# Blocks 2 to 6 of a fused attention and MLP layer: the second norm by row group, heads normalized by pairs, no held-back products

## The chip, the core and the metric

The kernel runs on one core of a Trainium2 chip. Its engines work from queues of their own, each in order: PE (TensorE, with its weight loads as PEld), DVE (VectorE), ACT (ScalarE), POOL (GpSimd), and SP, which issues nearly all transfers. They meet through semaphores. The metric is the device time of one execution in microseconds (us). The kernel before takes 1557.15 us, the median of three runs (1557.05 to 1557.82).

## The reference, cut to what matters

Sequence 2048, width 512, 32 heads of width 16 with one key and one value head for all, MLP width 1376.

```python
mod = silu(c) @ w_mod                       # six rows of 512: sa, ca, ga, sb, cb, gb
h = layernorm(x) * (1 + ca) + sa
q, k, v = h @ wq, h @ wk, h @ wv            # 32 query heads, one k and one v of width 16
p = softmax(q @ k.T / 4)                    # per head, 2048 x 2048
x = x + ga * ((p @ v) @ wo)
h = layernorm(x) * (1 + cb) + sb            # "the second norm"
x = x + gb * (gelu(h @ w1 + b1) @ w2 + b2)
```

Everything is fp32. Where a product of the projections and the MLP is made, each factor is split into a high and a low part in fp32r, and three matmuls (high by high, low by high, high by low) are summed; below, each of these matmuls counts as one product.

## The kernel before, in words

**Blocks, units, iterations.** The 2048 query rows are worked off in 8 blocks of 256 rows, numbered 0 to 7, and a block in 8 units of 4 heads. The main loop runs over the 64 units, four iterations to a unit: 256 iterations, 32 to a block. An iteration has two halves. In each half PE computes four score tiles transposed (`e`, line 615) for ACT to exponentiate (`p`, line 619), four score tiles in rows (`m`, line 510) of a unit some way ahead, of which DVE takes the maximum (`mx`, line 515), and at its end 16 matmuls of the probabilities with the values (`acc`, line 636). So two groups of 16 `acc` matmuls mark an iteration in the trace. The `e` and `m` tiles use 64 of the 128 rows of the array each, and two such matmuls can run side by side. From the 250th iteration on no `m` tiles are left; the loop then calls `alone`, and an iteration holds only `e`, `acc` and plain full-height matmuls. These are called the bare iterations.

**Batches.** What a block needs after its attention (the output projection, the second norm, the MLP) is written as a generator, `rest_steps`, which is fed into the iterations of the next block. It hands over batches of matmuls. One iteration takes at most one batch: six products of 512 columns (or twelve of 256), whose contraction is cut in two halves of 64 rows; one half runs beside the `e` and `m` tiles of the first half of the iteration, the other in the second. Batches of at most four products make an iteration of a shorter kind. An iteration without a batch is written by `plain`. The generator may also `yield` a number: it then rests for that many ticks of the variable `clock`, which counts four ticks to an iteration. `later(n, fn)` issues the instructions of `fn` after `n` ticks. Each engine's queue stands in the order that these calls give; nothing is moved afterwards.

**PSUM banks.** `m` tiles have three banks (tag "m"). A sum of the rest (`wops`, `tp`, `w1ps`, `w2ps`) has the bank "x". In an iteration without a batch, one `m` tile of each half goes to "x" (line 1447), so that four are then in use. A bank is free again when DVE has read it.

**The rest of a block, in order.** The output projection (`wops`) makes two row groups of 128 rows, two batches of six products in each of four iterations in all. DVE adds a row group to x (`add_x`, line 814). Then the second norm: `stats` (line 821, two instructions of 256 columns per row group), `rstd` (line 825: `bn_aggr` on DVE, line 827, then `ve`, line 828, and the power, line 830, on POOL), `xhat` on POOL (line 833), `add_bias` on POOL (line 837). In the kernel before, `rstd` is issued for both row groups together, and the generator rests 8 ticks, two iterations. Then two batches of four transposes (`tp`), the modulation on POOL, eleven tiles of the first MLP product (`w1ps`) with the gelu on DVE, ACT and POOL, and the second product (`w2ps`), 33 products for each of two row groups.

**Held-back products.** For blocks 4 and 5 (`held_back`, line 1045) the second row group stops 12 products short; the last 12 (`LATER = 4`) are made in two batches after the next block's output projection, in the two iterations in which that block's norm would otherwise leave none. A set `projected` says when.

**Heads.** Each head's sums must divide its outputs before the output projection. For blocks below `EARLY` this is done for the whole block after its last unit (`fetch`, line 726). From block `EARLY` on it is done by pairs of units while the block still runs (`finish_unit`, from line 664): `fetch_sums`, `invert_sums` (a reciprocal on DVE, line 676), `collect`, `scale_heads` on POOL (line 689). `EARLY` is 5 before.

**The end.** Block 6's last products are spread with `LONE` (how many of eleven k tiles of its first row group are made before the bare iterations) and batches of `SHORT` = 4 in the bare ones. What is left after the loop is given out by `some(n)` between the steps of block 7's norm: `TAIL[0]` products ahead of the first row group's transposes, `TAIL[1]` ahead of the second's, `TAIL[2]` ahead of the modulation.

Of the kernel before, what the change touches and what calls it, by code (L numbers as in the profile page):

```python
# [32 lines left out]
BUSY = 5  # L33
BATCH = 6
SHORT = 4
LONG = (3, 1)
TAIL = (11, 7, 6)
EARLY = 5
HELD = 4
LATER = 4  # L40
LONE = 5
SOON = 6
GROUP = 4
NORM_WAIT = 6
# [10 lines left out]
def adaln_mqa_mlp(  # L55
# [16 lines left out]
    _, S, D = x.shape  # L72
# [10 lines left out]
    NF = (F + P - 1) // P  # L83
# [710 lines left out]
    def rest_steps(b, fast, rp, bank, ons, ready):  # L794
# [4 lines left out]
        for hf in range(w // HQ):  # L799
# [20 lines left out]
            def stats(t, h):  # L820
                nc.vector.bn_stats(out=st[:, t, h, :], in_=x1[:, t, h * D // 2:(h + 1) * D // 2])  # L821
# [30 lines left out]
            if fast:  # L852
                turned = [psum.tile([P, HQ], F32, name=f"turned{q}", **bank()) for q in range(2)]
                rows_o = rp.tile([P, HQ], F32, name="rows_o", tag="rb", bufs=2)
                inv = att.tile([P, H * w // P], F32, name="inv", tag="rsum", bufs=1)

                def turn_o(q):
                    for t in range(2):
                        nc.tensor.transpose(turned[q][:, t * P:(t + 1) * P], ocs[q][:, t * P:(t + 1) * P], ident)

                def scale_o(q):
                    src = turned[q].rearrange("p (t c r) -> p t c r", t=2, c=4)
                    by = inv[:, 8 * q:8 * q + 8].rearrange("p (t c) -> p t c", t=2)
# [24 lines left out]
            else:  # L888
                for t in range(2):
                    ps = out_sum(t)  # L890
                    yield from batches(ps, out_pairs(t, range(KD)), BATCH, lambda g: b < EARLY or g in on_early[b][1])
                    add_x(t, ps)

                    for h in range(2):
                        later(3 - 2 * t + 2 * h, lambda t=t, h=h: stats(t, h))
                projected.add(b)
            if not fast:
                later(4, lambda: rstd(0, 2))
                later(5, lambda: xhat(0))
                later(5, lambda: xhat(1))  # L900
                later(9, lambda: add_bias(0))
                later(9, lambda: add_bias(1))

                later(BUSY, lambda: state.update(busy=True))
                yield 8
            hH = att.tile([P, KD, HQ], F32R, name=f"h2H{b}_{hf}", tag="xH", bufs=2)
            hL = att.tile([P, KD, HQ], F32R, name=f"h2L{b}_{hf}", tag="xL", bufs=2)

# [133 lines left out]

            while weights:
                yield 2
            held_back = not fast and EARLY <= b + 1 < len(blocks) - 1
            full = slice(0, D)
            parts = [(0, full), (1, slice(0, D // 2)), (1, slice(D // 2, D))] if fast else [(0, full), (1, full), (1, full)]
            sums = {}

            def second(n, fs, begin=True, end=True, put=store):  # L1050
                t, cols = parts[n]
                sl = slice(t * P, (t + 1) * P)
                if n not in sums:
                    place = dict(tag="m", bufs=3) if b == len(blocks) - 2 and t else bank()
                    sums[n] = psum.tile([P, D], F32, name=f"w2ps{b}_{hf}_{n}", **place)
                ops = [(gH[:, f, sl], gL[:, f, sl], w2H[:, f, cols], w2L[:, f, cols]) for f in fs]
                size_ = SHORT if b == len(blocks) - 2 and (t or not begin) else BATCH
                yield from batches(sums[n][:, :cols.stop - cols.start], ops, size_,
                                   lambda k: made.issuperset(range(fs[k] + 1)), begin, end)
                if not end:  # L1060
                    return
                if fast:
                    later(1, lambda: put(t, sums[n], cols))
                    yield 2
                else:
                    put(t, sums[n])
# [23 lines left out]
    projected = set()  # L1090
    drm = tc.dram_tile([4, D], F32, name="drm")

    mod_state = {}
# [487 lines left out]
```

## Time and profile before

| what | us |
|---|---|
| median of three runs | 1557.15 |
| the profiled execution | 1557.11 |
| its span, first to last instruction | 1555.3 |
| PE busy | 1539.4 (99%) |
| DVE busy | 1397.8 (90%) |
| ACT busy | 1230.8 (79%) |
| POOL busy | 685.5 (44%) |

The profiled execution's own time is 0.04 us below the median, so sums made against one hold for the other; 1.8 us of it lie around the span. The granted TensorE clock is 1.00 over the loop. A row of the timeline gives the start, how long it took, the engine, the line, the operation, what it writes and reads, and how many like instructions are merged in it (x2); in brackets stands how long the engine was idle ahead of it, and who released it. Matmuls overlap in the records: how fast PE goes is read from the distance between starts, not from the durations.

### The profile page before, as it was taken

What the parts mean: (1) busy time and instruction counts of PE and PEld (TensorE: products, weight loads), DVE (VectorE), ACT (ScalarE), POOL (GpSimd) and SP (SyncE); (2) the same over time, 40 slices, a digit from 0 to 9 for tenths busy, and PEclk for the clock granted to TensorE, in tenths of its full rate; (3) what the DMA queues carried; (4) which work ended last, traced back from release to release, by engine and by line L of the source; (5) the groups of instructions that cost most, each with busy time, mean ns of one, the idle gap of its engine ahead of it and who ended that gap; (6) DMA issues with size and microseconds to landing.
All of it is one profiled execution on the core that took longest, in us unless ns stands there. A gap on an engine that the chain in (4) does not pass through costs nothing.

```text
span 1555.3 us, 41563 instructions
## 1 busy us (share of the span) xinstructions
PE 1539.4 (99%) x16405; PEld 954.2 (61%) x16405; DVE 1397.8 (90%) x2488; ACT 1230.8 (79%) x2401; POOL 685.5 (44%) x1206
## 2 busy tenths in 40 slices
PE   7999999999999999999999999999999999999999
PEld 4455555567655665557655676556655676566658
DVE  7999999999999999999999999999999999999814
ACT  5577778788877887788877888788877888778874
POOL 5535432867322571246521563235711574046511
PEclk9999999999999999999999999999999999999999
DMA  7226412312030211203112120302102220202141
GB/s 248 94 88 200 151 57 83 127 51 97 18 106 25 74 67 37 93 19 109 33 51 79 56 87 16 111 26 93 62 31 73 65 96 24 87 28 99 48 150 48
DMA packets 84215, 120.85 MB, mean 78 GB/s; under 512 B 21342, under 2 KB 57438, under 8 KB 83764
## 3 DMA queue, kind: packets, MB, share of 16 engines
q1 hardware_dynamic: 84004, 118.18, 22.9%
q8 instruction: 130, 2.13, 0.6%
q14 instruction: 65, 0.53, 0.1%
q10 hardware_dynamic: 16, 0.00, 0.0%
HBM read 90.87 MB, written 26.74 MB: 76 GB/s over the span
## 4 chain that ended last, share of the span: by engine, by line
PE 90%; DVE 7%; DMA 1%; ACT 0%; issue 0%; POOL 0%; SPq 0%; ACTq 0%; DVEq 0%
PE acc L636 31%; PE m L510 25%; PE e L615 17%; PE w1ps L196 8%; DVE mx L515 6%; PE w2ps L186 2%; PE w2ps L196 2%; PE qps L196 1%; DMA xt<-in_A_x_dram 1%; PE w1ps L186 1%; PE wops L196 1%; PE tp L196 1%; PE kps L165 1%; DVE st L821 0%; DVE x L814 0%; PE wops L186 0%
## 5 line engine op out<-in xcount | busy, mean ns | idle before, releaser
L515 DVE TENSOR_REDUCE mx<-m 128x1 f32<-128x512 f32 x2048 | 1269.6, 681 | 88.1 <-PE m L510 65.0
L619 ACT ACTIVATE p<-e 128x512 f32<-128x512 f32 x2048 | 1099.0, 597 | 255.2 <-PE e L615 116.3
L510 PE MATMUL m<-ks,qst 64*128 64x512 f32 x2048 | 836.8, 429 | 2.0 <-DVE mx L515 0.6
L615 PE MATMUL e<-qst,ks 64*128 64x512 f32 x2048 | 740.4, 411 | 0.1
L636 PE MATMUL acc<-p,va 128*32 128x256 f32 x8192 | 548.0, 385 | 0.0
L510 PEld LDWEIGHTS m<-ks,qst 64*128 64x128 f32 x2048 | 367.4, 184 | 211.1 <-DVE mx L515 174.3
L615 PEld LDWEIGHTS e<-qst,ks 64*128 64x128 f32 x2048 | 359.3, 184 | 89.5 <-ACT p L619 61.8
L636 PEld LDWEIGHTS acc<-p,va 128*32 128x32 f32 x8192 | 213.8, 109 | 214.6 <-issue 111.6
L196 PE MATMUL w1ps<-h2H,w1t 64*128 64x256 f32 x1232 | 235.7, 287 | 0.0
L558 POOL TENSOR_SCALAR mt<-turned 8x32 f32<-8x32 f32 x256 | 53.3, 208 | 401.6 <-DVE turned L564 389.5
L196 PEld LDWEIGHTS w1ps<-h2H,w1t 64*128 64x128 f32 x1232 | 185.9, 185 | 28.9 <-DVE mx L515 14.8
L196 PE MATMUL w1ps<-h2L,w1t 64*128 64x256 f32 x616 | 169.3, 275 | 0.0
L196 PE MATMUL w2ps<-w2H,gH 64*128 64x512 f32 x274 | 120.3, 439 | 0.0
L196 PEld LDWEIGHTS w1ps<-h2L,w1t 64*128 64x128 f32 x616 | 113.6, 184 | 0.0
L196 PE MATMUL w2ps<-w2L,gH 64*128 64x512 f32 x274 | 107.4, 392 | 0.0
L196 PE MATMUL w2ps<-w2H,gL 64*128 64x512 f32 x274 | 106.9, 390 | 0.0
L973 POOL TENSOR_SCALAR tt<-tt 128x256 f32<-128x256 f32 x77 | 31.2, 405 | 130.9 <-ACT tt L972 96.0
L140 POOL TENSOR_TENSOR gL<-z,gH 128x256 fp32r<-128x256 f32 x77 | 57.2, 743 | 6.4
L974 POOL TENSOR_TENSOR tt<-tt,z 128x256 f32<-128x256 f32 x77 | 57.0, 740 | 6.4
L984 POOL TENSOR_TENSOR z<-tt,z 128x256 f32<-128x256 f32 x77 | 56.6, 735 | 6.0
L983 POOL TENSOR_TENSOR tt<-tt,z 128x256 f32<-128x256 f32 x77 | 56.7, 736 | 0.0
L196 PEld LDWEIGHTS w2ps<-w2H,gL 64*128 64x128 f32 x274 | 50.8, 185 | 0.9
(193 smaller groups left out, 1503.3 us busy)
## 6 DMA issues: line engine op xcount, KB each, us to landing
w1t<-dw SPq DMA_DIRECT2D x82, 512.0 KB
qst<-dq SPq DMA_DIRECT2D x384, 32.0 KB
do<-oc SPq DMA_DIRECT2D x62, 128.0 KB
dw<-w1s SPq DMA_DIRECT2D x11, 512.0 KB
xt<-in_A_x_dram SPq DMA_DIRECT2D x4, 1024.0 KB
dq<-qH SPq DMA_DIRECT2D x16, 256.0 KB
dq<-qL SPq DMA_DIRECT2D x16, 256.0 KB
x<-in_A_x_dram SPq DMA_DIRECT2D x8, 512.0 KB
```

Of the source, the lines that this page charges most:

```text
L140: eng_l.tensor_tensor(out=dst_l, in0=src, in1=raw(dst_h), op=ALU.subtract)
L186: nc.tensor.matmul(ps, a, b_, start=first_, stop=last_)
L196: ins = nc.tensor.matmul(ps, a[rows], b_[rows], start=first_ and s == 0, stop=last_ and s == 1)
L510: nc.tensor.matmul(m, qsts[u][rows, j, t * P:(t + 1) * P], ks[rows, kc * 512:(kc + 1) * 512], start=True, stop=True)
L515: nc.vector.tensor_reduce(out=self.mx[u][:, i, kc:kc + 1], in_=m, axis=AX.X, op=ALU.max)
L558: nc.gpsimd.tensor_scalar(out=mt[:, g:g + 32], in0=turned[g:g + 4 * T, :], scalar1=1.0, scalar2=0.0, op0=ALU.mult, op1=ALU.add)
L615: nc.tensor.matmul(e, ks[rows, kt * P:(kt + 1) * P], rhs, start=True, stop=True)
L619: ins = nc.scalar.activation(dst, e, AF.Exp, scale=0.25)
L636: ins = nc.tensor.matmul(accs[u][32 * cidx:32 * cidx + 32, :], va[:, kt, :], rhs, start=kt == 0, stop=kt == NKT - 1)
L974: nc.gpsimd.tensor_tensor(out=tt, in0=tt, in1=z, op=ALU.mult)
L983: nc.gpsimd.tensor_tensor(out=tt, in0=tt, in1=z, op=ALU.mult)
L984: nc.gpsimd.tensor_tensor(out=z, in0=tt, in1=z, op=ALU.add)
```

## The change

It does three things, for blocks 2 to 6.

1. The second norm is made per row group. `rstd`, `xhat` and `add_bias` of the first row group are issued while the second is still being projected; those of the second follow 1, 2 and 3 ticks after its addition. The generator rests 4 ticks, one iteration (two halves), and not 8.
2. `EARLY` goes from 5 to 2, so blocks 2, 3 and 4 too have their heads normalized by pairs of units.
3. No products are held back: `held_back`, `LATER` and `projected` are gone, and the second row group of blocks 4 and 5 is made in one go.

The numbers that spread the last products change with it: `LONE` 5 to 7, batches of `FEW` = 3 for the rest of block 6's first row group, and `TAIL` from (11, 7, 6) to (11, 4, 5).

```diff
-TAIL = (11, 7, 6)
-EARLY = 5
+TAIL = (11, 4, 5)
+EARLY = 2
 HELD = 4
-LATER = 4
-LONE = 5
+LONE = 7
+FEW = 3
...
                     for h in range(2):
-                        later(3 - 2 * t + 2 * h, lambda t=t, h=h: stats(t, h))
-                projected.add(b)
+                        if b < EARLY:
+                            later(3 - 2 * t + 2 * h, lambda t=t, h=h: stats(t, h))
+                        else:
+                            later(1 if t else 3 + 2 * h, lambda t=t, h=h: stats(t, h))
+                    if b >= EARLY:
+                        later(1 if t else 6, lambda t=t: rstd(t, t + 1))
+                        later(2 if t else 7, lambda t=t: xhat(t))
+                        later(3 if t else 8, lambda t=t: add_bias(t))
             if not fast:
-                later(4, lambda: rstd(0, 2))
-                later(5, lambda: xhat(0))
-                later(5, lambda: xhat(1))
-                later(9, lambda: add_bias(0))
-                later(9, lambda: add_bias(1))
-
-                later(BUSY, lambda: state.update(busy=True))
-                yield 8
+                if b < EARLY:
+                    later(4, lambda: rstd(0, 2))
...
+                later(BUSY if b < EARLY else 1, lambda: state.update(busy=True))
+                yield 8 if b < EARLY else 4
...
-            held_back = not fast and EARLY <= b + 1 < len(blocks) - 1
...
-                size_ = SHORT if b == len(blocks) - 2 and (t or not begin) else BATCH
...
-            elif held_back:
-                yield from second(0, range(NF))
-                yield from second(1, range(NF - LATER), put=add_x)
-                while b + 1 not in projected:
-                    yield 1
-                yield from second(2, range(NF - LATER, NF))
             elif b == len(blocks) - 2:
                 yield from second(0, range(LONE), end=False)
-                yield from second(0, range(LONE, NF), begin=False)
-                yield from second(1, range(NF))
+                yield from second(0, range(LONE, NF), begin=False, size_=FEW)
+                yield from second(1, range(NF), size_=SHORT)
```

Three places in the order of the instructions show what moves.

DVE, block 3, from the addition of its second row group on (`x` is the addition, `st` the statistics, `mv` the aggregate, `mx` a maximum over one `m` tile, whose index ahead of the running number, 0 or 1, names its half of the array; `mm` and `turned` are the last steps of a unit's maxima). Before:

```order
L814 TENSOR_TENSOR x_3_13119<-wops_0_1_13291,x_3_13119 128x512
L515 TENSOR_REDUCE mx_13393<-m_0_0_2_0_13457 128x1
L515 TENSOR_REDUCE mx_13393<-m_0_0_3_0_13468 128x1
L821 BN_STATS st_0_13128<-x_3_13119 128x6
L515 TENSOR_REDUCE mx_13393<-m_0_1_0_1_13486 128x1
L515 TENSOR_REDUCE mx_13393<-m_0_1_0_0_13489 128x1
L515 TENSOR_REDUCE mx_13393<-m_0_1_1_0_13495 128x1
L515 TENSOR_REDUCE mx_13393<-m_0_1_1_1_13498 128x1
L821 BN_STATS st_0_13128<-x_3_13119 128x6
L827 BN_AGGR mv_0_13129<-st_0_13128 128x2 x2
```

In the changed kernel:

```order
L814 TENSOR_TENSOR x_3_13117<-wops_0_1_13294,x_3_13117 128x512
L515 TENSOR_REDUCE mx_13143<-m_1_1_2_0_13460 128x1
L515 TENSOR_REDUCE mx_13143<-m_1_1_3_0_13471 128x1
L821 BN_STATS st_0_13126<-x_3_13117 128x6 x2
L827 BN_AGGR mv_0_13127<-st_0_13126 128x2
L515 TENSOR_REDUCE mx_13500<-m_0_0_0_1_13501 128x1
L515 TENSOR_REDUCE mx_13500<-m_0_0_0_0_13504 128x1
L515 TENSOR_REDUCE mx_13500<-m_0_0_1_0_13510 128x1
L515 TENSOR_REDUCE mx_13500<-m_0_0_1_1_13513 128x1
L563 TENSOR_REDUCE mm_194<-mx_13143 128x8
L564 STREAM_TRANSPOSE turned_13474<-mm_194 128x32
```

Both statistics and the aggregate now stand ahead of the first maximum of the iteration without a batch. In block 3 the unit boundary (`mm`, `turned`) falls into that iteration too; in blocks 2 and 6 a reciprocal of a pair's sums stands ahead of the statistics.

POOL, block 2, from the gather of a unit's maxima on (`mt`, `mh`, `ml`) to the modulation. Before:

```order
L558 TENSOR_SCALAR mt_10416<-turned_10415 8x32 x4
L133 TENSOR_SCALAR mh_10417<-mt_10416 8x128
L140 TENSOR_TENSOR ml_10418<-mt_10416,mh_10417 8x128
L828 TENSOR_SCALAR ve_0_10167<-mv_0_10165 128x2
L830 TENSOR_TENSOR rs_0_10166<-ve_0_10167,mhalf 128x2
L833 TENSOR_SCALAR xh_2_0_10163<-x_2_10155,mv_0_10165,rs_0_10166 128x512 x2
L837 TENSOR_TENSOR x_2_10155<-x_2_10155,b2g 128x512 x2
```

In the changed kernel:

```order
L833 TENSOR_SCALAR xh_2_0_10200<-x_2_10192,mv_0_10202,rs_0_10203 128x512
L837 TENSOR_TENSOR x_2_10192<-x_2_10192,b2g 128x512
L558 TENSOR_SCALAR mt_10456<-turned_10455 8x32 x4
L133 TENSOR_SCALAR mh_10457<-mt_10456 8x128
L140 TENSOR_TENSOR ml_10458<-mt_10456,mh_10457 8x128
L828 TENSOR_SCALAR ve_0_10204<-mv_0_10202 128x1
L830 TENSOR_TENSOR rs_0_10203<-ve_0_10204,mhalf 128x1
L833 TENSOR_SCALAR xh_2_0_10200<-x_2_10192,mv_0_10202,rs_0_10203 128x512
L837 TENSOR_TENSOR x_2_10192<-x_2_10192,b2g 128x512
L689 TENSOR_TENSOR os_10066<-os_10066 128x256
```

The first row group's normalization and bias now stand ahead of the gather, so that the second's is all that is left behind the last addition; a scaling of the next block's first pair (`os`) follows it.

PE, block 6, from the end of its output projection on. Before, the held-back products of block 5 (`w2ps_0_2`) follow:

```order
L636 MATMUL acc_22038<-p_966,va 32x256 x8
L196 MATMUL w2ps_0_2_22126<-w2H,gH_0_19632 128x512
L510 MATMUL m_0_1_0_1_22139<-ks,qst_160 128x512
L615 MATMUL e_4_0_1_22142<-qst_158,ks 128x512
L196 MATMUL w2ps_0_2_22126<-w2H,gL_0_19633 128x512
L510 MATMUL m_0_1_1_1_22146<-ks,qst_160 128x512
```

In the changed kernel:

```order
L636 MATMUL acc_22172<-p_966,va 32x256 x8
L615 MATMUL e_4_0_1_22281<-qst_158,ks 128x512
L615 MATMUL e_4_0_0_22284<-qst_158,ks 128x512
L510 MATMUL m_0_1_0_1_22287<-ks,qst_160 128x512
L510 MATMUL m_0_1_0_0_22290<-ks,qst_160 128x512
L615 MATMUL e_4_1_1_22293<-qst_158,ks 128x512
```

The iteration behind the projection holds no batch; the one after it holds the transposes.

Counted over the whole order: iterations without a batch inside the rest were two each in blocks 2, 3 and 4 and none in blocks 5 and 6; they are one each in blocks 2 to 6. Block 6's first row group has one more batch of six ahead of the bare iterations. The seven bare iterations hold 2, 4, 4, 4, 4, 5, 4 products before and 3, 3, 3, 3, 5, 4, 4 now, and 24 products were left after the loop, where 20 are now.

More of the change, by code (lines that the diff above doesn't have):

```diff
@@ L894, in rest_steps @@
                     for h in range(2):
-                        later(3 - 2 * t + 2 * h, lambda t=t, h=h: stats(t, h))
-                projected.add(b)
-            if not fast:
-                later(4, lambda: rstd(0, 2))
-                later(5, lambda: xhat(0))
-                later(5, lambda: xhat(1))
-                later(9, lambda: add_bias(0))
-                later(9, lambda: add_bias(1))
-                later(BUSY, lambda: state.update(busy=True))
-                yield 8
+                        if b < EARLY:
[6 more added lines that the diff above has]
+                        later(3 if t else 8, lambda t=t: add_bias(t))
+            if not fast:
+                if b < EARLY:
+                    later(4, lambda: rstd(0, 2))
+                    later(5, lambda: xhat(0))
+                    later(5, lambda: xhat(1))
+                    later(9, lambda: add_bias(0))
+                    later(9, lambda: add_bias(1))
+                later(BUSY if b < EARLY else 1, lambda: state.update(busy=True))
+                yield 8 if b < EARLY else 4
             hH = att.tile([P, KD, HQ], F32R, name=f"h2H{b}_{hf}", tag="xH", bufs=2)
@@ L1044, in rest_steps, with second @@
                 yield 2
-            held_back = not fast and EARLY <= b + 1 < len(blocks) - 1
             full = slice(0, D)
-            parts = [(0, full), (1, slice(0, D // 2)), (1, slice(D // 2, D))] if fast else [(0, full), (1, full), (1, full)]
+            parts = [(0, full), (1, slice(0, D // 2)), (1, slice(D // 2, D))] if fast else [(0, full), (1, full)]
             sums = {}
-            def second(n, fs, begin=True, end=True, put=store):
+            def second(n, fs, begin=True, end=True, size_=BATCH):
                 t, cols = parts[n]
@@ L1062, in second @@
                 if fast:
-                    later(1, lambda: put(t, sums[n], cols))
+                    later(1, lambda: store(t, sums[n], cols))
                     yield 2
                 else:
-                    put(t, sums[n])
+                    store(t, sums[n])
             if fast:
@@ L1089, in adaln_mqa_mlp @@
     stage = {}
-    projected = set()
     drm = tc.dram_tile([4, D], F32, name="drm")
```

## The prediction

> **What bounds the kernel now.** I read the page's busy times first, then the busy times by stage, then the timelines of PE and DVE through block 3's second norm, its neighbourhood in block 6, the bare iterations and the end.
>
> ```profile
> PE 1539.4 (99%) x16405; PEld 954.2 (61%) x16405; DVE 1397.8 (90%) x2488; ACT 1230.8 (79%) x2401; POOL 685.5 (44%) x1206
> 667.00:847.00 180.00, 179.91 (x2014) 112.47 (x2014) 168.55 (x296) 147.57 (x289) 74.11 (x139) 1.00 0.19 61
> 847.00:863.00 16.00, 15.90 (x163) 8.70 (x160) 15.78 (x29) 12.95 (x27) 8.75 (x10) 1.00 0.06 15
> ```
>
> The columns of the last two are the stretch, its length, and busy PE, PEld, DVE, ACT, POOL. PE has work at all times. DVE is busy for 94% (168.55 of 180) of a whole block, but for 99% (15.78 of 16) of the stretch behind the second row group's addition, the place that the change shortens by an iteration. There DVE has no slack:
>
> ```profile
> 845.86 0.17 DVE L563 TENSOR_REDUCE mm<-mx 128x8 f32<-128x32 f32 x1
> 846.30 1.29 DVE L515 TENSOR_REDUCE mx<-m 128x1 f32<-128x512 f32 x2
> 847.50 0.68 DVE L814 TENSOR_TENSOR x<-wops,x 128x512 f32<-128x512 f32 x1
> 848.10 1.28 DVE L515 TENSOR_REDUCE mx<-m 128x1 f32<-128x512 f32 x2
> 849.30 0.41 DVE L821 BATCH_NORM_STATS2 st<-x 128x6 f32<-128x256 f32 x1
> 849.63 2.46 DVE L515 TENSOR_REDUCE mx<-m 128x1 f32<-128x512 f32 x4
> 852.01 0.41 DVE L821 BATCH_NORM_STATS2 st<-x 128x6 f32<-128x256 f32 x1
> 852.35 0.32 DVE L827 BATCH_NORM_AGGREGATE mv<-st 128x2 f32<-128x12 f32 x2
> 852.59 9.60 DVE L515 TENSOR_REDUCE mx<-m 128x1 f32<-128x512 f32 x16
> ```
>
> Sixteen maxima follow each other in 9.60, 0.60 from start to start. A statistic costs 0.33 (849.30 to 849.63), two aggregates 0.24, so one 0.12; the unit boundary costs 0.44 (845.86 to 846.30).
>
> ```profile
> 847.60 1.07 PE L636 MATMUL acc<-p,va 128*32 128x256 f32 x16
> 850.21 1.07 PE L636 MATMUL acc<-p,va 128*32 128x256 f32 x16
> 851.78 0.86 PE L510 MATMUL m<-ks,qst 64*128 64x512 f32 x2
> 852.82 1.07 PE L636 MATMUL acc<-p,va 128*32 128x256 f32 x16
> 854.47 1.09 PE L510 MATMUL m<-ks,qst 64*128 64x512 f32 x2
> 855.50 1.07 PE L636 MATMUL acc<-p,va 128*32 128x256 f32 x16
> 858.12 1.07 PE L636 MATMUL acc<-p,va 128*32 128x256 f32 x16
> 859.46 0.38 PE L196 MATMUL tp<-ident,xh 64*128 64x128 f32 x2
> 860.45 0.50 PE L510 MATMUL m<-ks,qst 64*128 64x512 f32 x1
> 860.88 1.07 PE L636 MATMUL acc<-p,va 128*32 128x256 f32 x16
> ```
>
> The `acc` rows part the halves. The two iterations without a batch take 5.22 (847.60 to 852.82) and 5.30 (to 858.12). Four maxima run from 849.63 to 852.09, and the last `m` tile of the half ends at 852.64 (851.78 + 0.86), so it started at 852.15, with a matmul of 0.49: with four banks, the fourth tile of a half waits until DVE has read the fourth of the half before. The same holds at 855.56 (854.47 + 1.09) against the fourth reduction behind 852.59, done at 855.07 (four times 0.60 and the last one's end, 0.08 behind); that half is 2.68 long where others are 2.61. So PE is the bound on paper, and DVE paces it through the banks wherever it is late.
>
> **The change part by part.** *One more full iteration.* Six iterations without a batch become five, and block 6 puts one more batch of six ahead of the bare iterations.
>
> ```profile
> 1471.46 1.07 PE L636 MATMUL acc<-p,va 128*32 128x256 f32 x16
> 1474.31 1.07 PE L636 MATMUL acc<-p,va 128*32 128x256 f32 x16
> ...
> 1478.50 1.07 PE L636 MATMUL acc<-p,va 128*32 128x256 f32 x16
> 1480.83 1.07 PE L636 MATMUL acc<-p,va 128*32 128x256 f32 x16
> ```
>
> A half with a batch takes 2.85 (1471.46 to 1474.31), an iteration 5.70, so the exchange costs 5.70 - 5.22 = +0.5.
>
> *The bare iterations.* Two halves with one product each take 4.19 (1474.31 to 1478.50), 2.10 apiece; one with two takes 2.33. Two products fewer: 2 x 0.23 = -0.45.
>
> *No held-back products.* In block 6 they follow directly on the projection, and DVE's late start shows at once:
>
> ```profile
> 1368.40 0.23 DVE L676 RECIPROCAL sums<-sums 64x16 f32<-64x16 f32 x1
> 1368.56 0.36 DVE L821 BATCH_NORM_STATS2 st<-x 128x6 f32<-128x256 f32 x1
> 1368.85 2.45 DVE L515 TENSOR_REDUCE mx<-m 128x1 f32<-128x512 f32 x4
> ```
>
> ```profile
> 1366.71 1.07 PE L636 MATMUL acc<-p,va 128*32 128x256 f32 x16
> 1369.55 0.50 PE L510 MATMUL m<-ks,qst 64*128 64x512 f32 x1
> 1369.98 1.07 PE L636 MATMUL acc<-p,va 128*32 128x256 f32 x16
> 1372.90 1.07 PE L636 MATMUL acc<-p,va 128*32 128x256 f32 x16
> ```
>
> The fourth `m` tile starts at 1369.55, when the first of the four maxima from 1368.85 is done (here only three banks are in use). The halves take 3.27 and 2.92 against 2.85: 0.49 too long. Two such places go: -1.0. (A reciprocal costs 0.16, 1368.40 to 1368.56.)
>
> *The wait that takes their place.* Now the lone iteration without a batch comes with all statistics ahead of its first maximum. In block 3's rows: the first maximum starts not at 849.63 but after two statistics and an aggregate, 849.30 + 0.33 + 0.33 + 0.12 = 850.1, 0.47 later. The fourth `m` tile of the second half starts 0.47 later, and the half ends 0.24 later, since 0.23 of it lay beside the last `e` tile (from such a tile to the next `acc` row it takes 0.43, as 860.45 to 860.88 shows; 852.15 + 0.43 = 852.58 against 852.82). The iteration that gave DVE room to catch up is gone, so the transposes come at once. There, too, the fourth `m` tile (860.45) waits for DVE, and by the same sum ends its half another 0.24 later. That is 0.48 for a block without anything more (block 4 +0.08 from its unit boundary: 0.56). A reciprocal ahead of the statistics and the first aggregate, moved ahead too, add 0.28 in blocks 2 and 6: 0.76 each. In block 3 the unit boundary and a reciprocal fall between the lone iteration's maxima and the transposes' first one: 0.6 more, 1.08. In block 5 boundary, reciprocal, statistics and aggregate all fall into one projection iteration, about 0.4 more: 0.88. Together 4.0. Off goes what the second iteration lost before (5.30 against 5.22, three blocks): -0.25. These are estimates from the distances above. For their ends: nothing but the 0.08 of before in each block (0.4), and all five like block 3 with a reciprocal of 0.16 (6.2). I take 4.0, since the bank rule places each of the waits quoted to within 0.1.
>
> The Trainium skill ("VectorE: DVE Perf Modes", section "The DRAIN you can't avoid") says that the next VectorE instruction does not start until the pipeline of the one before has emptied. By it each maximum would hold DVE for its whole 0.68, and four of them would make every one of these waits 0.3 longer, some 3 us over ten half iterations (an estimate). The 16 maxima in 9.60 disagree: the next starts 0.08 ahead of the end.
>
> *POOL and the transposes.* The second row group's normalization starts after its aggregate:
>
> ```profile
> 853.91 4.16 POOL L833 TENSOR_SCALAR xh<-x,mv,rs 128x512 f32<-128x512 f32 x2
> ```
>
> One row group takes 2.08. From the aggregates' end (852.35 + 0.32 = 852.67) to it were 1.24; now the aggregate ends at 850.2, so the row is done by 850.2 + 1.24 + 2.08 = 853.5. The transposes move from 859.46 to 859.46 - 5.30 + 0.24 = 854.4. So they wait for nothing, with 0.9 to spare; cost 0. Late next would be the modulation, whose distance from the transposes stays.
>
> *Heads by pairs in blocks 2 to 4.* Per block eight reciprocals of 0.16 for one, on DVE, and 20 more transfers on SP. Blocks 5 to 7 bear the same before, and their iterations with a batch take the same 2.85 a half (the rows from 1471.46 are block 7's). Zero beside the reciprocals costed above; if that cover fails, three blocks times seven times 0.16 is +3.4.
>
> *The end.* The products left go from 24 to 20.
>
> ```profile
> 1515.08 0.39 PE L186 MATMUL w2ps<-w2H,gH 128*128 128x512 f32 x1
> 1517.38 0.40 PE L186 MATMUL w2ps<-w2H,gL 128*128 128x512 f32 x1
> 1519.80 0.60 PE L929 MATMUL tp<-ident,xh 128*128 128x128 f32 x4
> 1521.63 0.40 PE L186 MATMUL w1ps<-h2H,w1t 128*128 128x256 f32 x2
> ```
>
> ```profile
> 1518.10 0.55 DVE L833 TENSOR_SCALAR xh<-x,mv,rs 128x512 f32<-128x512 f32 x1 [0.46 <-POOL rs L830]
> 1521.15 0.43 DVE L140 TENSOR_TENSOR h2L<-h,h2H 128x256 fp32r<-128x256 f32 x1
> ```
>
> Eleven products start from 1515.08 to 1517.38, 0.23 apart. Three fewer ahead of the second transposes move these from 1519.80 to 1519.11, still behind their input (1518.65). One fewer behind: the first MLP matmul comes at 1520.7, its third at 1520.9, when the low part, moved along, is done (1521.58 - 0.69 = 1520.89). Just covered: 4 x 0.23 = -0.9; at worst 0, if the norm's latency takes the place.
>
> Sum: +0.5 - 0.45 - 1.0 + 4.0 - 0.25 + 0 - 0.9 = +1.9. From the profiled 1557.11 (0.04 below the median) that gives 1559.0 us.
>
> **Rivals.** *PE alone sets the pace.* If the lateness of DVE is absorbed, the wait term is 0.4 and the sum -1.7: 1555.4. For it speak PE's 99%, and the two iterations of 5.22 and 5.30, nearly equal although the first holds all the statistics; against it the 3.27 half. The Trainium skill ("Perfetto Trace Analysis", section "Identifying the Most-Contended Engine") says that matmul busy time is no good measure of how close TensorE is to its limit, since matmuls are pipelined. By that rule the 99% counts for nothing here, and the sum with DVE's lateness, 1559.0, stands against 1555.4. The 3.27 half agrees: PE is shown busy in it.
>
> *The transposes wait for POOL.* This ends on the slow side. Where the first row group's bias (half of two, 1.27 each) or a gather of maxima stands ahead and is late, the second normalization slips. It decides from 0.9 on; a bias and a gather together would be some 3, so 2 in each of five blocks: +10, 1569. POOL's 44% and the first group's early start speak against it.
>
> *The fewer leftovers do nothing at the end,* because the norm's latency fills the hole: +0.9 on the sum, 1559.9. The input of the second transposes, 0.46 early even then, speaks against it.
>
> **How the numbers follow.** Chances: the sum with DVE's lateness 0.57, PE alone 0.23, POOL 0.10, the end 0.10. 0.2%, 3.1 us, is about what a measurement of this kernel can tell from no change: 1554.0 to 1560.3. Of PE alone I put 0.07 beyond 1554.0 (the held-back places may have cost more), of the main case 0.15 beyond 1560.3, all of POOL and 0.03 of the end: faster 0.07, slower 0.28, same 0.65. The range reaches down to PE alone, 1555.2, and up to 1562.2, the wait term's upper end (+2.2) with 1.0 for reciprocals less well covered; outside lie POOL and the edge of PE alone.
>
> **What would show it.** In the changed kernel: one iteration without a batch in each of blocks 2 to 6, 5.4 to 5.7 long, and a first half with transposes of 3.0 (3.6 in block 3) where it was 2.76 (858.12 to 860.88); `m` matmuls there starting as a maximum ends; transposes 0.5 or more behind the end of `xh`; halves of 2.85 elsewhere; the first `w1ps` of block 7 some 0.9 sooner after the loop. I am wrong if the lone iteration takes 5.2 (PE alone), or if PE idles ahead of `tp` (POOL).

## The result and the profile after

The changed kernel takes 1560.11 us (median of 20 runs, 1558.62 to 1561.38), the kernel before 1557.13 (20 runs, 1556.53 to 1558.28): ratio 1.0018, 95% interval 1.0011 to 1.0025. Beside the experiments, on another chip, it took 1559.27 against 1557.54: 1.0012 (1.0003 to 1.0021). So it is slower by 2 to 3 us: both intervals leave out no change, and both ratios lie under the 0.2% that the prediction took for what a measurement can tell. The forecast was 1559.0, in a range of 1555.2 to 1562.2.

The profiled run of after took 1558.62 us (span 1556.8) and was the shortest of its 20, 1.5 below the median; the profiled run of before sat at its median. A part of what the shortest run lacked is found below.

The page of after, busy times; then, by stretch (columns as in the prediction), block 3 behind the second row group's addition:

```profile
PE 1540.1 (99%) x16411; PEld 954.9 (61%) x16411; DVE 1398.3 (90%) x2507; ACT 1230.8 (79%) x2401; POOL 690.7 (44%) x1234
```

```profile
843.90:855.70 11.80, 11.48 (x116) 6.54 (x112) 11.43 (x24) 8.78 (x18) 5.74 (x10) 1.00 0.08 25
```

As sums they tell almost nothing: over the whole span PE and DVE are as busy as before to within 1 us, and in the short stretch both are busy for 97% (11.48 and 11.43 of 11.80). The change is seen in the order. Timeline of after on DVE, block 3:

```profile
844.73 0.74 DVE L821 BATCH_NORM_STATS2 st<-x 128x6 f32<-128x256 f32 x2
845.50 0.21 DVE L827 BATCH_NORM_AGGREGATE mv<-st 128x2 f32<-128x12 f32 x1
845.63 2.43 DVE L515 TENSOR_REDUCE mx<-m 128x1 f32<-128x512 f32 x4
...
850.75 0.23 DVE L676 RECIPROCAL sums<-sums 64x16 f32<-64x16 f32 x1
850.91 2.41 DVE L515 TENSOR_REDUCE mx<-m 128x1 f32<-128x512 f32 x4
```

The same stretch on PE, and the second row group's normalization on POOL, in blocks 3 and 4:

```profile
843.04 1.07 PE L636 MATMUL acc<-p,va 128*32 128x256 f32 x16
845.64 1.07 PE L636 MATMUL acc<-p,va 128*32 128x256 f32 x16
848.55 1.07 PE L636 MATMUL acc<-p,va 128*32 128x256 f32 x16
849.89 0.38 PE L196 MATMUL tp<-ident,xh 64*128 64x128 f32 x2
851.58 0.50 PE L510 MATMUL m<-ks,qst 64*128 64x512 f32 x1 [0.20 <-DVE mx L515]
852.01 1.07 PE L636 MATMUL acc<-p,va 128*32 128x256 f32 x16
```

```profile
846.79 2.09 POOL L833 TENSOR_SCALAR xh<-x,mv,rs 128x512 f32<-128x512 f32 x1
...
1022.80 2.09 POOL L833 TENSOR_SCALAR xh<-x,mv,rs 128x512 f32<-128x512 f32 x1
```

The lone iteration (the one without a batch behind the projection) takes 2.60 + 2.91 = 5.51 (before 5.22). Its second half and the first half with transposes, 3.46 (before 2.76), end late, because the fourth `m` tile waits for a maximum. In the transposes' half the profile names DVE at 851.58, and that maximum is the first of the four from 850.91; in the lone half the tile starts at 848.11, and the four maxima from 845.63 end at 848.06. The transposes start 1.0 us behind the end of `xh` (848.88).

In block 4, where no reciprocal falls in, the halves from the addition on are 2.61, 2.89 and 2.98. The timeline of after on PE, there, in the bare iterations and at the end:

```profile
1019.05 1.07 PE L636 MATMUL acc<-p,va 128*32 128x256 f32 x16
1021.66 1.07 PE L636 MATMUL acc<-p,va 128*32 128x256 f32 x16
1024.55 1.07 PE L636 MATMUL acc<-p,va 128*32 128x256 f32 x16
1027.53 1.07 PE L636 MATMUL acc<-p,va 128*32 128x256 f32 x16
...
1477.21 1.07 PE L636 MATMUL acc<-p,va 128*32 128x256 f32 x16
1479.31 1.07 PE L636 MATMUL acc<-p,va 128*32 128x256 f32 x16
1481.64 1.07 PE L636 MATMUL acc<-p,va 128*32 128x256 f32 x16
...
1509.09 1.96 PE L636 MATMUL acc<-p,va 128*32 128x256 f32 x32
1523.16 0.40 PE L186 MATMUL w1ps<-h2H,w1t 128*128 128x256 f32 x2
```

Before, the loop's last `acc` row is this one:

```profile
1506.66 1.95 PE L636 MATMUL acc<-p,va 128*32 128x256 f32 x32
```

A bare iteration takes 2.10 + 2.33 = 4.43 (before 4.65). From the loop's last `acc` row to block 7's first `w1ps` it takes 14.07 us, before 14.97 (1521.63 - 1506.66): 0.90 less.

### The profile page after: what moved, and what is told of

Same layout as the page of the kernel before. It is cut to its first block, busy times and chain, and to the rows that moved or that the text cites. A ratio compares the mean times of both kernels' runs of the same rounds, so it can differ in the third digit from the quotient of the medians.

```text
span 1556.8 us, 41726 instructions
## 1 busy us (share of the span) xinstructions
PE 1540.1 (99%) x16411; PEld 954.9 (61%) x16411; DVE 1398.3 (90%) x2507; ACT 1230.8 (79%) x2401; POOL 690.7 (44%) x1234
## 4 chain that ended last, share of the span: by engine, by line
PE 90%; DVE 7%; DMA 1%; ACT 1%; issue 0%; POOL 0%; SPq 0%; DVEq 0%
PE acc L636 31%; PE m L510 26%; PE e L615 17%; PE w1ps L196 8%; DVE mx L515 6%; PE w2ps L186 2%; PE qps L196 1%; PE wops L196 1%; DMA xt<-in_A_x_dram 1%; PE w1ps L186 1%; PE w2ps L196 1%; PE kps L165 1%; PE tp L196 1%; DVE st L821 0%; DVE x L814 0%; PE wops L186 0%
```

## The experiments

Each was timed beside the kernel before on the same chip; kernels of one group share it.

| kernel | us, median | ratio to before | 95% interval |
|---|---|---|---|
| *group 1, before 1557.54* | | | |
| after, again | 1559.27 | 1.0012 | 1.0003 to 1.0021 |
| after, narrow statistics | 1557.33 | 0.9999 | 0.9990 to 1.0008 |
| after, doubled statistics | 1564.37 | 1.0047 | 1.0035 to 1.0060 |
| after, one product twice | 1559.31 | 1.0011 | 1.0002 to 1.0020 |
| *group 2, before 1557.27* | | | |
| before, heads by pairs | 1557.85 | 1.0006 | 0.9998 to 1.0014 |
| after, first reciprocals later | 1558.44 | 1.0009 | 1.0000 to 1.0018 |
| after, all reciprocals later | 1563.47 | 1.0032 | 1.0020 to 1.0044 |
| after, late statistics | 1561.89 | 1.0027 | 1.0018 to 1.0036 |
| *group 3, before 1558.04* | | | |
| after, late statistics, split `xh` | 1560.14 | 1.0013 | 1.0004 to 1.0022 |
| the same, first reciprocals later | 1559.28 | 1.0006 | 0.9998 to 1.0015 |
| the same, pairs from block 3 | 1558.90 | 1.0002 | 0.9993 to 1.0011 |

### Is it DVE's lateness, or PE alone?

*The changed kernel again.*

> The changed kernel once more, unaltered, for a second profile of it. Its first profile (1558.62 us) is the shortest of its runs, 1.5 us below their median of 1560.11, so some waits that the median run has may be missing there. If the lateness of VectorE is the whole story, the lone iterations and the first ones with transposes take again 5.5 to 5.6 and 5.7 to 6.2, and a longer run shows its extra 1 to 2 us as PE waiting for a transfer or for one particular engine at a place that can be named. If the extra is spread over all iterations alike, no place will show it. Time 1560.1, against the kernel before +3.0.

1559.27 us. The lone and the transposes' iterations came out within 0.02 of the first profile. The profiled run took 1559.98, 1.36 more than the first one. Of these, 0.59 lie ahead of the loop (its first `e` matmul starts at 75.32, in the first profile at 74.73), and 0.76 at one place that has a name. Timeline of this run on DVE, on PE and on SP, at block 4's first unit:

```profile
828.75 0.25 DVE L676 RECIPROCAL sums<-sums 64x16 f32<-64x16 f32 x1 [1.08 <-DMA sums<-do]
```

```profile
829.59 0.49 PE L510 MATMUL m<-ks,qst 64*128 64x512 f32 x1 [0.27 <-DVE mx L515]
```

```profile
819.77 0.43 SPq L788 DMA_DIRECT2D x<-in_A_x_dram  x1
820.24 1.44 SPq L782 DMA_DIRECT2D w1t<-dw  x3
821.78 0.57 SPq L673 DMA_DIRECT2D sums<-do  x1
```

The 4 KB of sums for the reciprocal were asked for at 821.78, behind 2 MB of rows and weights (four transfers of 512 KB), and landed 6.4 us after the issue ended. DVE had nothing ahead of it that could run: the reciprocal stood first in its queue, and the maxima that PE needs stood behind. That half iteration is 0.76 us longer than in the first profile, where DVE idled 0.13 at this place; in five more profiles of kernels that leave this place as it is, DVE idled 0.76 to 1.55.

The Trainium skill ("DMA: Bandwidth & Descriptors", section "Queues, rings and completion order") says that on each DMA engine the descriptors of a queue are consumed in ring order. The 6.4 us for 4 KB agree: 2 MB went ahead on the same queue. The same transfer in before, where no load stood ahead of it, landed 1.4 us after the end of its issue (1476.65 against 1474.69 + 0.58), and here too DVE was waiting for it. Timeline of before on SP and DVE:

```profile
1474.69 0.58 SPq L673 DMA_DIRECT2D sums<-do  x1
```

```profile
1476.65 0.24 DVE L676 RECIPROCAL sums<-sums 64x16 f32<-64x16 f32 x1 [0.70 <-DMA sums<-do]
```

*Less work for DVE.*

```diff
-                nc.vector.bn_stats(out=st[:, t, h, :], in_=x1[:, t, h * D // 2:(h + 1) * D // 2])
+                wide = 32 if t and not fast and b >= EARLY else D // 2
+                nc.vector.bn_stats(out=st[:, t, h, :], in_=x1[:, t, h * D // 2:h * D // 2 + wide])
```

> The changed kernel with the second row group's two statistics of each of blocks 2 to 6 taken over 32 columns and not 256 (this leaves out most of that statistic, so the normalized rows are other numbers). Each statistic then costs VectorE an estimated 0.1 us where it cost 0.33, so it is about 0.46 us earlier at each of the five lone iterations. Lateness of VectorE: what the first reduction gains is what the lone iteration and the first one with transposes lose of their waits, up to 0.24 in each half iteration that waits: 0.4 to 0.5 for each block, -2.0 to -2.5 us in all, and lone iterations of about 5.3. PE alone sets the pace: no change, within 0.3 us. Transposes wait for POOL: mv is 0.46 earlier, so -2.3 us too, but then PE idles ahead of the transposes in the changed kernel, which its profile does not show.

1557.33, so 1.9 us under the changed kernel, just short of the 2.0 to 2.5 expected, and level with the kernel before. Timeline on PE, block 4:

```profile
1020.12 1.07 PE L636 MATMUL acc<-p,va 128*32 128x256 f32 x16
1022.73 1.07 PE L636 MATMUL acc<-p,va 128*32 128x256 f32 x16
1025.35 1.07 PE L636 MATMUL acc<-p,va 128*32 128x256 f32 x16
1028.16 1.07 PE L636 MATMUL acc<-p,va 128*32 128x256 f32 x16
```

The three halves take 2.61, 2.62 and 2.81: 8.04 where the changed kernel has 8.48. The work of PE is the same. The rival of PE alone, which allowed 0.3, falls.

*More work for DVE.*

```diff
-                nc.vector.bn_stats(...)
+                for _ in range(2 if t and not fast and b >= EARLY else 1):
+                    nc.vector.bn_stats(...)
```

> The changed kernel with the second row group's two statistics of each of blocks 2 to 6 issued twice, so VectorE is 0.66 us later at each lone iteration. Lateness of VectorE: the lone iteration already waits, so nothing covers this; up to 0.66 for each block, +3.3 us in all, less what the transposes' iteration has to spare; at least +2. PE alone: 0. POOL: the normalization comes 0.66 later too, less than the 0.9 that the prediction gave it to spare, so PE does not idle ahead of the transposes; if that spare time is smaller than it was worked out, PE idles there, and the total goes towards +5.

1564.37, so +5.1: the sign and the place as expected, the size half as much again. Timeline on DVE in block 3, and on PE:

```profile
847.18 1.67 DVE L822 BATCH_NORM_STATS2 st<-x 128x6 f32<-128x256 f32 x4
848.89 0.21 DVE L828 BATCH_NORM_AGGREGATE mv<-st 128x2 f32<-128x12 f32 x1
```

```profile
845.50 1.07 PE L636 MATMUL acc<-p,va 128*32 128x256 f32 x16
...
851.93 1.07 PE L636 MATMUL acc<-p,va 128*32 128x256 f32 x16
```

The aggregate comes 1.71 behind the first statistic, in the changed kernel 0.77 (845.50 - 844.73): 0.94 later and not 0.66. The lone iteration takes 6.43 (851.93 - 845.50), 0.92 more. What DVE is late there, PE is late, one to one. In the five blocks the lone iterations are 0.90 to 0.95 longer, 4.7 together, and block 3's first half with transposes another 0.30 (3.76 against 3.46): 5.0 of the 5.1.

*More work for PE.*

```diff
+            for _ in range(2 if self.twice else 1):
                 nc.tensor.matmul(m, qsts[u][rows, j, t * P:(t + 1) * P], ...)
+            self.twice = False
...
```

> The changed kernel with one maximum-finding product (m) of the second half of each lone iteration of blocks 2 to 6 issued twice: PE gets about 0.23 us more work in each, 1.15 us in all, and VectorE none. Lateness of VectorE: PE waits there for a bank anyway, so the added product lies inside the wait or, where its tile comes behind the wait, adds its 0.23: between 0 and +0.5 us. PE alone sets the pace: the full +1.15 us.

1559.31: +0.04 on the changed kernel, and no lone iteration differs by more than 0.02. Five products more cost nothing: PE had room for them. That they lie inside the wait fits, but is not shown apart from the other reading, that they run beside a tile on the other half of the array.

### What do heads by pairs cost?

```diff
+PAIRS = 2
-        if b < EARLY:
+        if b < PAIRS:
```

(in the kernel before, at the three places where heads by pairs are chosen)

> The kernel before with one part of the change alone: the heads are normalized by pairs from block 2 on. The prediction put this part at nothing, with +3.4 us as the end of its range (three blocks, seven more reciprocals of 0.16 us). Since then the second profile of the changed kernel shows VectorE idle for 1.08 us at 828.75 us, ahead of block 4's first reciprocal, until the 4 KB of sums have landed that were asked for behind block 3's weights. If the prediction's cover holds: 0, within 0.4 us. If the reciprocals are uncovered where the iteration is full, and the wait for the sums comes in this kernel as well: +0.6 for the iterations of blocks 2 to 4 that got 0.1 longer each, and 0.3 to 1.5 more for the wait, so +0.9 to +2.1 us.

1557.85: +0.6 us, 95% interval -0.3 to +2.2, so the time alone does not tell it from nothing. The profile says where it would come from: six half iterations of blocks 2 to 4 are 0.09 to 0.13 longer than in before, 0.62 together, three of them those with a block's first reciprocal. (The profiled run took 1561.70; 2.85 of that lie ahead of the loop, whose first `e` matmul starts at 78.08, in before at 75.23.) So the reciprocals seem not fully covered, and the wait for the sums is absent. Timeline of this kernel on SP, the same unit:

```profile
823.16 0.58 SPq L674 DMA_DIRECT2D sums<-do  x1
823.79 0.45 SPq L789 DMA_DIRECT2D x<-in_A_x_dram  x1
824.29 1.96 SPq L783 DMA_DIRECT2D w1t<-dw  x3
```

Here the sums go ahead of the 2 MB, since the loads fall elsewhere against the units. The wait in block 4 comes of heads by pairs and the changed kernel's order together; before has no such reciprocal there, and this kernel no wait for it.

*The first unit's reciprocal later.*

```diff
-        later(4 if Q == NQ - 1 else 6, invert_sums)
+        later(4 if Q == NQ - 1 else 6 if Q else 8, invert_sums)
```

> The changed kernel with the reciprocal of the first unit of each block (heads by pairs) two half cycles later, nothing else moved. If VectorE, with its in-order queue, waits there for the transfer of the sums (1.08 us in the second profile of the changed kernel, 1.55 and 1.46 in those of the two kernels with other statistics, 0.13 in the first one), that wait goes, the PE's wait of the same place goes with it, and the time falls by about 1 us against the changed kernel of 1559.3: some 1558.3. If the first profile, without the wait, is the rule and the extra of the median sits elsewhere: no change.

1558.44, near the expected 1558.3: DVE does not wait for these sums in its profile, and the kernel stands 1.2 us above its kernel before, where the changed kernel stands 1.7 (group 1) or 3.0. The intervals overlap, so the size is not settled, but the wait is gone from where it was. A part of the gain is not that wait: against the first profile, which hardly had it, the half iterations of the projection that held a block's first reciprocal are 0.09 to 0.10 shorter in four blocks.

*All reciprocals later.*

```diff
-        later(4 if Q == NQ - 1 else 6, invert_sums)
+        later(4 if Q == NQ - 1 else 8, invert_sums)
```

> The changed kernel with every reciprocal of the head sums two half cycles later, but the one of each block's last unit. Beside the wait for the first unit's sums (about -1 us, as with the first unit's alone), this takes the reciprocal of 0.16 us out of the neighbourhood of the lone iterations of blocks 2, 3 and 6. Lateness of VectorE: up to 0.16 less in each of the two half iterations that wait there, so -0.3 to -0.9 us more than with the first unit's alone. PE alone: no more than with the first unit's alone.

1563.47: the expectation was wrong. The kernel stands 6.2 us above its kernel before, the changed kernel 1.7 to 3.0. Around 900 us the timeline of the changed kernel on SP reads

```profile
897.38 0.60 SPq L685 DMA_DIRECT2D os<-drs  x1
...
906.36 0.82 SPq L782 DMA_DIRECT2D w1t<-dw  x2
```

and this kernel's, followed by what PE waits for:

```profile
901.20 0.60 SPq L685 DMA_DIRECT2D os<-drs  x1
...
909.67 0.91 SPq L782 DMA_DIRECT2D w1t<-dw  x2
```

```profile
913.22 0.63 PE L636 MATMUL acc<-p,va 128*32 128x256 f32 x6 [1.57 <-DMA w1t<-dw]
```

The inverse sums go out to DRAM and come back, and SP now stands 2.3 us on the way back, with the maxima's rows and the weights behind it in its queue. The weights are asked for 3.3 us later, and PE waits 1.57 for them. Against the first profile of the changed kernel, the half iteration with this wait is 2.17 longer, and those at the same stage of the next three blocks 0.75, 0.64 and 0.55. Together these are 4.1, and the two profiled runs lie 3.9 apart. For the last two of the four the profile names no wait for the weights, so their cause goes by their place alone. The expectation had counted DVE alone and no queue.

### The price of late transposes, and whether the wait can be moved

```diff
-                            later(1 if t else 3 + 2 * h, lambda t=t, h=h: stats(t, h))
+                            later(3 - 2 * t + 2 * h, lambda t=t, h=h: stats(t, h))
-                        later(1 if t else 6, lambda t=t: rstd(t, t + 1))
-                        later(2 if t else 7, lambda t=t: xhat(t))
-                        later(3 if t else 8, lambda t=t: add_bias(t))
+                        later(3 if t else 6, lambda t=t: rstd(t, t + 1))
+                        later(3 if t else 7, lambda t=t: xhat(t))
+                        later(4 if t else 8, lambda t=t: add_bias(t))
```

> The changed kernel with the second row group's statistics where the kernel before had them, two half cycles apart, so that the normalization on POOL starts later by about 2.1 us while the transposes stay. This puts a price on the rival in which the transposes wait for POOL. The changed kernel's transposes start 1.0 us behind the end of xh. If that is time to spare, PE idles ahead of the transposes for 2.1 - 1.0 = 1.1 us in each of five blocks, and VectorE's lateness at the lone iteration (0.3 to 0.45 a block by the kernel with narrow statistics) goes: +3 to +4 us in all against the changed kernel. If a part of the 1.0 us is needed for the hand-over from POOL to PE, PE idles for up to 2.1 us a block: +8 us. If POOL's row of xh is no condition of the transposes' time at all, the time falls by 1.5 to 2 us.

1561.89: 4.6 us above its kernel before, where the changed kernel stands 1.7 (group 1), so about 2.9 for the edit, just under the 3 to 4 expected. Timeline on POOL and PE, block 4:

```profile
1027.10 2.09 POOL L833 TENSOR_SCALAR xh<-x,mv,rs 128x512 f32<-128x512 f32 x1
```

```profile
1020.95 1.07 PE L636 MATMUL acc<-p,va 128*32 128x256 f32 x16
1023.55 1.07 PE L636 MATMUL acc<-p,va 128*32 128x256 f32 x16
1026.16 1.07 PE L636 MATMUL acc<-p,va 128*32 128x256 f32 x16
...
1029.25 0.37 PE L196 MATMUL tp<-ident,xh 64*128 64x128 f32 x1 [0.70 <-POOL xh L833]
...
1030.12 1.07 PE L636 MATMUL acc<-p,va 128*32 128x256 f32 x16
```

The lone iteration is back at 5.21, and the half behind it takes 3.96. The fifth transpose, the first to read the second row group, goes 0.06 behind the end of `xh` (1029.19). From the `acc` row ahead of the transposes to the end of `xh` it takes 3.03 (1029.19 - 1026.16), in the changed kernel 0.34 (1024.89 - 1024.55), so 2.7 later. PE waits 0.70 of these 2.7, so the other 2.0 were time to spare.

*The same, with `xh` in two pieces.* The edit adds to the one above:

```diff
+                cols = D // 2 if t and not fast and b >= EARLY else D
+                for c in range(0, D, cols):
                     ...tensor_scalar(out=xh[:, t, c:c + cols], in0=x1[:, t, c:c + cols], ...)
```

> The changed kernel with the statistics of the second row group two half cycles apart, as in the kernel that priced POOL, and with that row group's normalization on POOL in two pieces of 256 columns. In the kernel with late statistics the first four transposes (row group 0) went at once, the fifth waited 0.70 us for the end of xh, and went 0.06 us behind it; the transposes of the first iteration read columns 0 to 255 alone. One piece is half of 2.09 us, so it ends about 1.0 us sooner than the whole did, and the fifth transpose finds it done, give or take 0.2. Lateness of VectorE as the cause of the longer lone iterations: they stay at the 5.2 us of the late statistics, the transposes' iterations come back to some 5.5 to 5.7, and the time falls by 0.3 to 0.6 us a block against the changed kernel: -1.5 to -3 us of 1559.3. If the lone iteration's wait only moves to the transposes' iteration, the time is that of the changed kernel.

1560.14, ratio 1.0013: the time of the changed kernel, so the gain of 1.5 to 3 us did not come, and the wait only moved. Timeline on PE and POOL, block 4:

```profile
1020.79 1.07 PE L636 MATMUL acc<-p,va 128*32 128x256 f32 x16
1023.40 1.07 PE L636 MATMUL acc<-p,va 128*32 128x256 f32 x16
1026.00 1.07 PE L636 MATMUL acc<-p,va 128*32 128x256 f32 x16
1029.28 1.07 PE L636 MATMUL acc<-p,va 128*32 128x256 f32 x16
```

```profile
1026.94 2.44 POOL L835 TENSOR_SCALAR xh<-x,mv,rs 128x256 f32<-128x256 f32 x2
```

The halves take 2.61, 2.60 and 3.28: 8.49, against 2.61, 2.89 and 2.98, which is 8.48. The profile names no wait of PE for `xh`, and what the lone iteration gained the next half gives back to the hundredth. In all five blocks the lone iteration lost 0.29 to 0.42 and the next one gained as much, within 0.02. DVE's work in the three halves is the same in both orders, and PE leaves them when DVE does: in the third half `m` tiles start at 1027.66, 1028.26 and 1028.86, each 0.05 or 0.06 behind the end of a maximum (1027.61, 1028.21, 1028.80). Only the kernel with narrow statistics, which does less, leaves them sooner.

*With the first unit's reciprocal later as well, and with pairs from block 3 on.* The edits are those above, put together.

> As the kernel with split normalization, and with the reciprocal of each block's first unit two half cycles later. The two causes, lateness of VectorE and the wait for the sums behind the weights, are at different places of the program, so they should add up: about 1 us less than with the split alone, 1555.5 to 1557, so equal to the kernel before or up to 0.1% faster than it. If they don't add, it is as fast as the better of the two, about 1557 to 1558.

> As the kernel with both mends, and with the heads of block 2 normalized by the four again, by pairs only from block 3 on. If the reciprocals of the pairs are not covered (single iterations of block 2 are 0.11 to 0.18 us longer in the changed kernel at four places, 0.6 in all), the time falls by 0.3 to 0.6 us more; if that was chance: no change, within 0.3.

1559.28 and 1558.90: -0.9 and another -0.4 in the same group. The 1555.5 to 1557 expected of the first was missed, since the split had given nothing to add to. What the two mends of the pairs give adds up, but the intervals overlap, and the 0.4 is not clear of noise. The second is level with the kernel before (its median 0.9 us above, ratio 1.0002, 0.9993 to 1.0011), so no version was found that beats it.

## Why the prediction was right, point by point

**The wait that takes the place of the removed one** (+4.0) was the step on which all hung, and it held in place, cause and, within 10%, in size. By block, lone iteration and first iteration with transposes against 5.22 and 5.48:

| block | predicted | in the profile of after |
|---|---|---|
| 2 | 0.76 | 0.41 + 0.22 = 0.63 |
| 3 | 1.08 | 0.29 + 0.70 = 0.99 |
| 4 | 0.56 | 0.29 + 0.28 = 0.57 |
| 5 | 0.88 | 0.30 + 0.22, and 0.34 in the projection iteration (6.12, before 5.78) = 0.86 |
| 6 | 0.76 | 0.41 + 0.22 = 0.63 |
| sum | 4.04 | 3.68 |

That the lone iterations wait for DVE is shown from both sides: narrow statistics took away all of their wait (0.27 to 0.41 a block) and 0.04 to 0.18 of the transposes', and doubled ones added 0.90 to 0.95. What is left of the transposes' wait, 0.53 in block 3, is put down to the unit boundary and the reciprocal by its place; moving the reciprocal away took off 0.10, and the boundary alone was not tried. What the step did not say: this is a debt that lies in no one iteration. The one other order tried (split `xh`) moved it and made it no smaller.

One wait was not foreseen. The second iteration with transposes of block 5 takes 5.78 against 5.48. It is not this step's: with narrow statistics its long half stays at 3.07, and with doubled ones, or with the first reciprocals later, that half takes 2.78. Its cause stays open.

**One more full iteration, bare iterations, end** (+0.5, -0.45, -0.9): +0.48 (an iteration of 5.68 to 5.70), -0.47 (seven iterations, 31.88 us against 32.35: 1477.21 to 1509.09, before 1474.31 to 1506.66) and -0.90. All as worked out; with the -0.90 the rival in which the fewer leftovers do nothing at the end falls. The second plain iterations that went were 5.28, 5.30 and 5.38 long, so -0.30 for -0.25.

**No held-back products** (-1.0): the two iterations were 6.11 and 6.19 against 5.70, and the ones with transposes behind them 5.71 and 5.58 against 5.48: -1.2. The cause, DVE's late start, is read from the profile; a kernel that drops the held-back products alone was not tried.

**POOL and the transposes** (0, with 0.9 to spare): right. The rival's place was right, its point, the first transpose, too early: with late statistics `xh` came 2.7 us later against its half and PE waited 0.70. It is the fifth transpose that needs the row.

**Heads by pairs** (0, bound +3.4): this step failed, as the cover was taken from blocks 5 to 7 and from full iterations. Alone the part costs some +0.6 (interval -0.3 to +2.2), and with the shorter norm it makes DVE wait for the sums behind 2 MB of weights, 0.1 us in the first profile, 0.8 to 1.6 in others. The step counted 20 more transfers on SP and did not ask where in SP's queue the one stands that a DVE instruction needs. In the second profile that is 0.76 of the 1.36 us by which it exceeds the first. Another 0.59 lies ahead of the loop, where the profiles of the changed kernel and its variants differ by 1.4 us (first `e` matmul at 74.54 to 75.97), and why is open.

In sum: 0.48 - 0.47 - 0.90 - 0.30 - 1.2 + 3.7 + 0.6 = +1.9, with block 5's unforeseen 0.3 it is +2.2, and the sums' wait comes on top: some +2 to +3, as measured. The first profile shows +1.5; its loop also began 0.5 us sooner (first `e` matmul at 74.73, before 75.23). That the parts add up to the forecast's +1.9 is in part luck: the wait came out 0.3 smaller and the held-back places 0.2 larger, and the pairs, forecast at nothing, made up for both.

**The rival of PE alone** is refuted by two runs, and a third agrees: less work for DVE is worth 1.9 us, more of it costs 5.1, and more work for PE nothing. **The rule on VectorE's emptied pipeline** was read too widely in the prediction. The same section of the Trainium skill ("VectorE: DVE Perf Modes", "The DRAIN you can't avoid") adds that an instruction that is not held starts earlier. Maxima, and statistics that write to different places, do (0.60 apart at 0.68 long); four statistics of which each second one writes where the first did take 1.67, 0.42 apiece at 0.41 long, and the aggregate (845.50) starts behind the end of the statistic that it reads (844.73 + 0.74).

## What to carry to other kernels

Where two engines are both nearly full, look in each stage at which of them leaves it last. Here another order only moved the wait from one iteration to the next, and only less work for that engine removed it. An instruction that waits for a transfer holds up all that stands behind it on its engine, so for each new one ask what stands ahead of its transfer in the queue, and what is queued behind the instruction. A cover that hides a cost in one stage is no evidence for another one.

## What had not been expected of the hardware

A transfer of 4 KB took 6.4 us from the end of its issue where 2 MB stood ahead of it on the same queue, and 1.4 us where nothing did. From run to run an engine that looked 90% busy idled between 0.1 and 1.6 us for it. In the rows read here, DVE overlaps neighbours by some 0.08 us where the second neither reads nor overwrites what the first writes, and not where it does: two statistics issued twice cost 0.94 more and not 0.66. POOL handed a row to PE within 0.06 us, and two pieces of 256 columns took POOL 2.44 us, where the whole row takes 2.09.
